# A list scheduler's prices: ScalarE, VectorE and GpSimd come free before an instruction's result, and exponentials are priced lower

## The chip, the cores and the metric

The kernel runs on one core of a Trainium2 chip. The metric is the device time of one execution in microseconds (us). TensorE (PE) multiplies matrices and loads its weights in a lane of its own (PEld); ScalarE (ACT), VectorE (DVE) and GpSimd (POOL) do elementwise work; SyncE (SP) only issues DMAs.

## What is computed

Local and global attention, then two MLP blocks, all in float32:

```python
scores = q @ k.T / sqrt(64) + bias               # 16 heads x 768 tokens, 8 global + 96 local keys
x = softmax(where(keep, scores, -1e9)) @ v
xk, xr = mu_k*x + (1-mu_k)*x_prev, mu_r*x + (1-mu_r)*x_prev
k = max(xk @ w_k, 0)                              # 512 -> 1024
x = sigmoid(xr @ w_r) * (k*k @ w_v)
xn = (x - mean) / sqrt(var + 1e-6) * g_ln
out = x + max(xn @ w_ch1, 0) @ w_ch2              # 512 -> 2048 -> 512
```

## The kernel before

The kernel has three stages. The **attention stage** (to about 148 us) goes through 12 blocks of 128 tokens, each in two halves of four heads. A half is: scores on PE (L484), four bias-and-minimum instructions on VectorE (L495, tile `t0l`), four exponentials on ScalarE (L501), transposes of the result on PE (L519), one copy `yy` on ScalarE (L337), and the product with the values on PE (L534), "values" below. Around each block PE also turns q and k (L438) and the reciprocal sums (L569); ScalarE copies the results (`b0h`, `xg`). In the same stage weights arrive by DMA and are converted and split into two float32r parts (L337, L341, L593 to L595, L601, L605), on ScalarE, VectorE and GpSimd. The first products of the first MLP, r (L720) and k of the first group (L756), can already run here, as fillers between the attention's PE work.

The **first MLP** (148 to about 282 us) is long runs of L756, L793 to L795 on PE. The **second MLP** (282 to 547 us) is 16 steps. A step has seven products P1 to P7 (L1047, six matmuls each, in the order P1 P6 P5 P7 P2 P4 P3) and three "down" groups of four operations (L1141 to L1143, three matmuls an operation). Between them, VectorE adds the products (L1055), ScalarE applies the ReLU and rounds the result to the high half of `h` (L1062, L337), and GpSimd makes the low half (L1066, four per step, called lows here; the fourth belongs to P3). A down group adds into banks 4 and 5 of PSUM, which VectorE's L1147 frees. In the even steps from 2 to 12 the weights of the next pair of steps are converted as well; on GpSimd that is a bundle of four small adds (L1000 to L1003) and two splits (L605) for each of two chunks.

The order of instructions on the four engines is not written by hand. `Plan.play` is a greedy list scheduler that runs when the program is built: it keeps a clock for each engine, and of all operations that can go it takes the one that can start first by these clocks; the due time only breaks ties. An operation names the engines that may do it with a price in ns on each; with two names, the engine that would finish first gets it, so prices also decide who does a conversion's copy (ScalarE 670 or GpSimd 850). A result may be used `LAG` = 70 ns after its end. Engines then run their instructions strictly in the order that came out. The lines that set a clock, and the price of an exponential:

```python
end = t + engines[e]
self.clock[e] = end
p.op({"ACT": 465 + 0.86 * w}, exp, ...)     # w = 128 or 232 columns
```

Of the kernel before, what the change touches and what calls it, by code (L numbers as in the profile page):

```python
# [51 lines left out]
def slope(h):  # L52
    return 2.0 ** (-8.0 * (h + 1) / H)
# [37 lines left out]
class Room:  # L91


    def __init__(self, tag, bufs, make, hold=False):
        self.tag, self.bufs, self.make, self.hold = tag, bufs, make, hold
        self.left, self.end, self.tile = 0, 0.0, None
# [13 lines left out]
class Plan:  # L110
# [4 lines left out]
    LAG = 70.0  # L115

    SWITCH = 95.0

    def __init__(self, clock):
        self.clock = {e: 1000.0 * t for e, t in clock.items()}  # L120
# [21 lines left out]
    def play(self):  # L142
        n = len(self.ops)
        wait = [len(x[2]) for x in self.ops]
        users = [[] for _ in self.ops]
        for i, x in enumerate(self.ops):
            for d in x[2]:
                users[d].append(i)
        ready = [0.0] * n
        by = {}  # L150
        free = {}
        live = {}
        open_ = [i for i in range(n) if not wait[i]]
        dma, mode = 0.0, ""
        trace = []
        while open_:
            best = None
            for i in open_:
                engines, _, _, rooms, due, _, _ = self.ops[i]
                at = ready[i]  # L160
                ok = True
                for x in rooms:
                    if x.tile is None:
                        if live.get(x.tag, 0) < x.bufs:
                            f = free.setdefault(x.tag, [0.0] * x.bufs)
                            at = max(at, f[0])
                        else:
                            ok = False
                if not ok:
                    continue  # L170
                for e, ns in engines.items():
                    t = max(at, self.clock[e])
                    if len(engines) > 1 and any(max(at, self.clock[g]) + m < t + ns for g, m in engines.items() if g != e):
                        continue
                    key = (t, due, i, e)
                    if best is None or key < best:
                        best = key
            if best is None:
                raise RuntimeError("no operation can go: " + str([(i, [x.tag for x in self.ops[i][3] if x.tile is None]) for i in open_][:20]))
            t, _, i, e = best  # L180
            engines, fn, _, rooms, _, size, way = self.ops[i]
            for x in rooms:
                if x.tile is None:
                    live[x.tag] = live.get(x.tag, 0) + 1
                    free[x.tag].pop(0)
                    x.tile = x.make()
            self.now = t
            fn(e)
            end = t + engines[e]
            if e == "PE" and way != mode:  # L190
                end += self.SWITCH
                mode = way
            self.clock[e] = end
            if size:
                dma = max(dma, end) + size / 190.0
                end = dma + 1900.0
            trace.append((t, end, e, i))
            for x in rooms:
                x.left -= 1
                x.end = max(x.end, end)  # L200
                if not x.left and not x.hold:
                    live[x.tag] -= 1
                    free[x.tag].append(x.end + self.LAG)
                    free[x.tag].sort()
            open_.remove(i)
            for u in users[i]:
                ready[u] = max(ready[u], end + self.LAG)
                wait[u] -= 1
                if not wait[u]:
                    open_.append(u)  # L210
        assert not any(wait), [i for i in range(n) if wait[i]][:20]
        return trace


class Fast:
# [247 lines left out]
    def plan_scores(self, i):  # L463


        nc, p = self.nc, self.plan
        n, hf = i // 2, i % 2
        c0, c1 = self.cols(n)
        w = c1 - c0
        banks = [Room(f"b{(2 * i + e) % 3}", 1, lambda e=e: self.bank((2 * i + e) % 3)) for e in range(2)]  # L470
        S = lambda k: banks[k % 2].tile[:, 0 : 2 * w].rearrange("p (j w) -> p j w", j=2)[:, k // 2, :]
        due = self.due(i)
        if hf == 0:
            self.sm[n] = self.room("sm", 3, [P, H])
        sm = self.sm[n]
        tp, mn = self.tp[i], _ = Part([self.TP, self.token(f"tp{i % 3}", 1)], lambda t, _: t[:, i % 3]), self.room("mn", 3, [P, 4])
        sides = [n % 2] if n % NB == 0 else [0, 1, 2]
        o = P + MAXG if n % 2 else 0
        s = hf if n == 0 else 0

        def scores(e):
            for k in range(4):
                r, c = slice((k % 2) * D, (k % 2 + 1) * D), 2 * hf + k // 2
                nc.tensor.matmul(S(k), self.qT(n)[r, c], self.kT()[r, c, c0:c1], start=True, stop=True)  # L484

        reads = self.sides(n, s, "qT", n % 2)
        for x in sides:
            reads += self.sides(n, s, "kT", x)
        p.op({"PE": 3.4 * w}, scores, reads, [("S", i)], banks + [self.Q, self.K], due, mode="rows")
        for x, k in enumerate((0, 2, 1, 3)):  # L490
            h = 4 * hf + k

            def least(e, k=k, h=h):
                bias = self.nb0 if n % NB == 0 else self.nb[:, o : o + WW]
                nc.vector.tensor_tensor_reduce(  # L495
                    tp.tile[:, k, 0:w], S(k), bias, slope(h), 3.0e38, ALU.add, ALU.min, mn.tile[:, k : k + 1]
                )

            def exp(e, k=k, h=h):
                t = tp.tile[:, k, 0:w]  # L500
                nc.scalar.activation(t, t, AF.Exp, bias=mn.tile[:, k : k + 1], scale=-1.0, accum_out=sm.tile[:, h : h + 1])  # L501

            p.op({"DVE": 165 + 1.31 * w}, least, [("S", i), ("nb", n % NB > 0)], [("tp", i, k)], [tp, mn, banks[k % 2], self.bias], due + 1 + x)
            p.op({"ACT": 465 + 0.86 * w}, exp, [], [("tp", i, k), ("sm", n, h)], [tp, mn, sm], due + 1.5 + x)

    def plan_weighted(self, i):

# [880 lines left out]
```

## Time and profile before

| | us |
|---|---|
| three timed runs | 554.62, 555.76, 554.92 (median 554.92) |
| the profiled execution | 556.07 |
| its span, first to last instruction | 554.2 |
| PE busy (3178 matmul records) | 528.0 (95%) |
| DVE, ACT, POOL busy | 403.8 (73%), 288.2 (52%), 278.6 (50%) |
| granted TensorE clock, mean | 0.989 |

The trace comes from the profiled execution, which took 1.15 us more than the median; 1.9 us of it lie outside the span. Times inside the trace count from the first instruction. A busy matmul is not a matmul at its peak, because matmuls overlap; so where PE's pace matters, the starts of two following instructions are compared, and not their durations.

### The profile page before, as it was taken

The page shows a single profiled execution, that of the slowest core. Times are in us where ns is not written, and L with a number is a line of the kernel's source. Part 1 is how long each engine was busy: PE and PEld are TensorE (multiplying, and loading weights), DVE is VectorE, ACT ScalarE, POOL GpSimd, SP SyncE. Part 2 cuts the span into 40 slices and gives each one's busy share as a digit, 9 for nine tenths or more (in the row PEclk, how much of TensorE's full clock was granted, in tenths as well). Part 3 has the DMA queues.
Part 4 walks back from the last instruction along what each step waited for, and adds up shares of the span by engine and source line. Part 5 has one row for each costly group of instructions (what it writes and reads, how often), then busy time and mean ns, then how long its engine had stood idle before and what let it go on. Part 6 is the DMA issues. An engine that isn't in the chain of part 4 may idle for free.

```text
span 554.2 us, 8779 instructions
## 1 busy us (share of the span) xinstructions
PE 528.0 (95%) x3178; PEld 454.2 (82%) x3178; DVE 403.8 (73%) x791; ACT 288.2 (52%) x641; POOL 278.6 (50%) x338
## 2 busy tenths in 40 slices
PE   5889999999999999999999999999999999999994
PEld 4667776887799898988888898788888889888983
DVE  4788799786597355828889987777676867867463
ACT  2687888777543313454446472473545526454320
POOL 3168575745545022151236592793855739585200
PEclk9699999999999999999999999999999999999999
DMA  8899667421310000020220123012130311311024
GB/s 168 205 229 192 150 157 176 146 69 53 101 38 2 1 2 0 1 72 5 77 69 8 52 63 95 20 64 90 45 109 0 115 39 43 110 38 39 0 77 157
DMA packets 59456, 42.64 MB, mean 77 GB/s; under 512 B 49036, under 2 KB 49292, under 8 KB 59404
## 3 DMA queue, kind: packets, MB, share of 16 engines
q1 hardware_dynamic: 58796, 41.33, 27.9%
q8 instruction: 27, 0.44, 0.3%
q10 hardware_dynamic: 576, 0.66, 0.3%
q14 instruction: 25, 0.20, 0.1%
q0 software_dynamic: 32, 0.00, 0.0%
HBM read 38.84 MB, written 3.15 MB: 76 GB/s over the span
## 4 chain that ended last, share of the span: by engine, by line


## 5 line engine op out<-in xcount | busy, mean ns | idle before, releaser
L1147 DVE TENSOR_TENSOR xg<-b,xg 128x1024 f32<-128x1024 f32 x44 | 53.6, 1219 | 39.5 <-PE b L1143 39.3
L595 DVE SCALAR_TENSOR_TENSOR cv<-cv,stage 128x512 int32<-128x512 int32 x50 | 43.9, 879 | 8.9 <-ACT cv L337 5.0
L594 DVE SCALAR_TENSOR_TENSOR stage<-stage 128x512 int32<-128x512 int32 x50 | 46.8, 938 | 0.6
L501 ACT ACTIVATE t0l<-t0l,mn 128x232 f32<-128x232 f32 (+1 forms) x96 | 44.5, 467 | 4.4 <-DVE mn L495 4.2
L1066 POOL TENSOR_TENSOR h<-rt,h 128x384 fp32r<-128x384 f32 x28 | 35.9, 1281 | 15.3 <-ACT h L337 15.3
L495 DVE CUSTOM_DVE_ANT_0 t0l<-b,ln 128x232 f32<-128x232 f32 (+1 forms) x96 | 32.0, 373 | 14.5 <-PE b L484 14.5
L664 POOL TENSOR_SCALAR rt<-xg,vec 128x256 f32<-128x256 f32 x48 | 29.9, 639 | 15.6 <-DVE m L771 4.3
L605 POOL TENSOR_TENSOR s<-cv,s 128x384 fp32r<-128x384 f32 (+1 forms) x22 | 26.8, 1217 | 19.0 <-ACT s L601 19.0
L1066 POOL TENSOR_TENSOR h<-e,h 128x384 fp32r<-128x384 f32 x14 | 15.9, 1134 | 38.2 <-ACT h L337 38.2
L831 POOL TENSOR_SCALAR st<-st 128x1 f32<-128x1 f32 x12 | 4.5, 375 | 60.2 <-DVE st L828 60.0
L756 PE MATMUL b<-b0l,t1l 128*128 128x256 f32 x144 | 32.6, 284 | 0.5 <-DVE rt L766 0.5
L593 DVE TENSOR_SCALAR stage<-stage 128x512 int32<-128x512 int32 x50 | 30.9, 620 | 2.8 <-DMA stage<-in_moe_w_v_dram 1.6
L519 PE MATMUL b<-ident,t0l 128*116 128x128 f32 (+1 forms) x176 | 30.1, 287 | 1.5 <-ACT t0l L501 1.5
L669 DVE SCALAR_TENSOR_TENSOR rt<-xg,vec,rt 128x256 f32<-128x256 f32 x48 | 29.1, 654 | 1.4 <-POOL rt L664 1.4
L1062 ACT ACTIVATE e<-e 128x384 f32<-128x384 f32 x16 | 8.3, 522 | 41.5 <-DVE e L1055 41.5
L534 PE MATMUL b<-yy,h 116*64 116x128 f32 (+1 forms) x352 | 25.0, 283 | 4.8 <-ACT yy L337 4.8
L1047 PE MATMUL b<-t1h,s 128*128 128x384 f32 x128 | 27.8, 339 | 0.6 <-DVE e L1055 0.6
L1062 ACT ACTIVATE rt<-rt 128x384 f32<-128x384 f32 x32 | 16.6, 520 | 22.6 <-DVE rt L1055 22.6
L534 PEld LDWEIGHTS b<-yy,h 116*64 116x64 f32 (+1 forms) x352 | 19.0, 138 | 11.2 <-ACT yy L337 8.6
L337 ACT ACTIVATE yy<-b 116x1024 f32<-116x1024 f32 (+1 forms) x24 | 22.8, 949 | 10.0 <-PE b L519 9.9
L1047 PE MATMUL b<-t0h,s 128*128 128x384 f32 x128 | 27.9, 339 | 0.0
L519 PEld LDWEIGHTS b<-ident,t0l 128*116 128x116 f32 (+1 forms) x176 | 20.1, 139 | 8.5 <-issue 3.8
(307 smaller groups left out, 1673.4 us busy)
## 6 DMA issues: line engine op xcount, KB each, us to landing
stage<-in_moe_w_ch_dram SPq DMA_DIRECT2D x32, 512.0 KB
stage<-in_moe_w_k_dram SPq DMA_DIRECT2D x8, 512.0 KB
stage<-in_moe_w_v_dram SPq DMA_DIRECT2D x8, 512.0 KB
h<-in_v_dram SPq DMA_DIRECT2D x10, 192.0 KB
b0l<-in_q_dram SPq DMA_DIRECT2D x7, 256.0 KB
out_dram<-xg SPq DMA_DIRECT2D x3, 512.0 KB
stage<-in_moe_w_r_dram SPq DMA_DIRECT2D x2, 512.0 KB
b0h<-in_q_dram SPq DMA_DIRECT2D x4, 256.0 KB
```

The costliest lines, as they stand in the source:

```text
L495: nc.vector.tensor_tensor_reduce(tp.tile[:, k, 0:w], S(k), bias, slope(h), 3.0e38, ALU.add, ALU.min, mn.tile[:, k : k + 1])
L501: nc.scalar.activation(t, t, AF.Exp, bias=mn.tile[:, k : k + 1], scale=-1.0, accum_out=sm.tile[:, h : h + 1])
L519: nc.tensor.transpose(b.tile[0:w, c, k * P : (k + 1) * P], tp.tile[:, k, c * w : (c + 1) * w], self.ident)
L534: nc.tensor.matmul(o, self.V[n].tile[0:w, c, h, :], y.tile[0:w, c, k * P : (k + 1) * P], start=c == 0, stop=c == m - 1)
L593: p.op({"DVE": 500}, lambda e: nc.vector.tensor_scalar(low(), low(), 29, None, ALU.logical_shift_right), [R], [(R, 1)], [raw], due - 2, be ...
L594: p.op({"DVE": 760}, lambda e: nc.vector.scalar_tensor_tensor(low(), high(), -(1 << 31), low(), ALU.bitwise_and, ALU.bitwise_or), [R, (R, ...
L595: p.op({"DVE": 760}, lambda e: nc.vector.scalar_tensor_tensor(y(), y(), 3, low(), ALU.logical_shift_left, ALU.bitwise_or), [(R, 2)], [C], ...
L664: nc.gpsimd.tensor_scalar(y.tile[:, u], z, v, 0.0, ALU.mult, ALU.add)
L756: nc.tensor.matmul(o, l, r, start=s == 0, stop=s == 11)
L1047: nc.tensor.matmul(acc(x), lhs(i, c, n), rhs(r, j, c), start=y == 0, stop=y == 5)
L1066: lambda e: (nc.vector if e == "DVE" else nc.gpsimd).tensor_tensor(o(1), V(y), o(0).bitcast(F32), ALU.subtract),
L1147: p.op({"DVE": 1250}, lambda e, x=x, z=rooms[0]: nc.vector.tensor_tensor(x(), z.tile.rearrange("p a n -> p (a n)"), x(), ALU.add), cells, ...
```

## The change

Two prices change and nothing else. After an operation, the clock of ScalarE, VectorE or GpSimd is set back by 105, 85 or 120 ns from the operation's end; the result still counts as ready at the end. And an exponential is priced 80 ns lower.

```diff
     SWITCH = 95.0
+    OVERLAP = {"ACT": 105.0, "DVE": 85.0, "POOL": 120.0}
...
-            self.clock[e] = end
+            self.clock[e] = end - self.OVERLAP.get(e, 0.0)
...
-            p.op({"ACT": 465 + 0.86 * w}, exp, [], [("tp", i, k), ("sm", n, h)], [tp, mn, sm], due + 1.5 + x)
+            p.op({"ACT": 385 + 0.86 * w}, exp, [], [("tp", i, k), ("sm", n, h)], [tp, mn, sm], due + 1.5 + x)
```

The same operations are built, 2142 in number; what moves is their order, on every engine, and for 22 operations the engine: 18 of them are copies of a weight conversion, ten from ScalarE to GpSimd and eight the other way. PE's 654 operations keep 89 changes between its kinds of work. Three places follow. In the changed kernel every line after 117 has a number one higher.

**Place 1: PE in the attention stage, around block 6's first scores.** Before, transposes of half 10 (L519), the turn of k for block 6 (L438), its scores (L484), another turn, then the values of half 10 (L534):

```order
L438 MATMUL b3_126_840<-ident_60,u_12_128 128x128 x4
L519 MATMUL b45_125_829<-ident_60,t0l_24_190 116x128 x2
L484 MATMUL b0_129_857<-b0h_15_139,b0l_11_126 128x128
L484 MATMUL b1_130_858<-b0h_15_139,b0l_11_126 128x128
...
L438 MATMUL b3_131_863<-ident_60,b0l_11_126 128x128 x4
L534 MATMUL b6_134_881<-yy_34_228,h1_13_135 64x128 x8
```

The same place of the changed kernel:

```order
L520 MATMUL b45_125_836<-ident_60,t0l_24_190 116x128 x6
L721 MATMUL b7_126_845<-s0_33_231,h0_70_463 128x512 x6
L439 MATMUL b3_130_863<-ident_60,u_12_128 128x128 x4
...
L520 MATMUL b45_125_836<-ident_60,t0l_24_190 116x128 x2
L485 MATMUL b0_131_888<-b0h_15_139,b0l_11_126 128x128
L485 MATMUL b1_132_889<-b0h_15_139,b0l_11_126 128x128
...
L721 MATMUL b7_134_899<-s0_33_231,h0_70_463 128x512 x6
L535 MATMUL b6_137_915<-yy_35_242,h1_13_135 64x128 x8
```

The r products of group 1 (L721), which stood some forty operations later before, now lie between these transposes, scores and values. All r and first k products are used up earlier: the last of them stands 27 places of PE's 654 earlier, and the last five halves of the attention have none between their operations.

**Place 2: PE in the second MLP, between the last down group of step 2 and the first of step 3.** Before, from the last matmul of step 2 (tile `h1_463`): P2 and P4 of step 4 (L1047), then step 3's first down operation (tile `h1_491`):

```order
L1143 MATMUL b45_489_3704<-b0r_325_2450,h1_463_3514 128x512
L1047 MATMUL b2_490_3719<-b0h_352_2685,s0_349_2668 128x384 x4
L1047 MATMUL b2_490_3719<-b0l_383_2975,s0_349_2668 128x384 x2
L1047 MATMUL b3_492_3732<-t0h_327_2468,s0_349_2668 128x384 x4
L1047 MATMUL b3_492_3732<-t0l_330_2481,s0_349_2668 128x384 x2
L1141 MATMUL b45_494_3747<-b1h_390_3041,h1_491_3726 128x512
L1142 MATMUL b45_494_3747<-yy_409_3171,h1_491_3726 128x512
L1143 MATMUL b45_494_3747<-b1h_390_3041,h1_491_3726 128x512
```

The same place of the changed kernel:

```order
L1144 MATMUL b45_484_3670<-b0r_325_2450,h1_461_3488 128x512
L1048 MATMUL b6_486_3690<-b0h_352_2678,s0_349_2665 128x384 x4
L1048 MATMUL b6_486_3690<-b0l_383_2976,s0_349_2665 128x384 x2
L1048 MATMUL b7_488_3703<-t0h_327_2468,s0_349_2665 128x384 x4
L1048 MATMUL b7_488_3703<-t0l_330_2478,s0_349_2665 128x384 x2
L1048 MATMUL b0_489_3713<-t0h_327_2468,s0_349_2665 128x384 x4
L1048 MATMUL b0_489_3713<-t0l_330_2478,s0_349_2665 128x384 x2
L1048 MATMUL b1_490_3721<-t0h_327_2468,s0_349_2665 128x384 x4
L1048 MATMUL b1_490_3721<-t0l_330_2478,s0_349_2665 128x384 x2
L1142 MATMUL b45_493_3733<-b1h_390_3043,h1_487_3697 128x512
L1143 MATMUL b45_493_3733<-yy_412_3181,h1_487_3697 128x512
L1144 MATMUL b45_493_3733<-b1h_390_3043,h1_487_3697 128x512
```

Four products (P1, P6, P5, P7 of step 4) instead of two now stand between the end of step 2 and step 3's first down operation. Step 2's last group itself stands four products earlier than before, and in later steps too the down groups follow their step's products more closely: in steps 8 and 12 the third down operation, which needs the low of P3, comes after P1, a down operation, P6, a down operation, P5 and P7.

**Place 3: GpSimd in step 8, ahead of the low of P3.** Before, the bundle of the first chunk and then the low (L1066):

```order
L1003 TENSOR_TENSOR stage_557_4216<-cv_574_4333,stage_557_4216 128x128
L605 TENSOR_TENSOR s1_395_3074<-cv_574_4333,s1_395_3074 128x384
L605 TENSOR_TENSOR s1_395_3074<-stage_557_4216,s1_395_3074 128x512
L1066 TENSOR_TENSOR h0_572_4319<-rt_569_4303,h0_572_4319 128x384
L1000 TENSOR_TENSOR stage_561_4253<-cv_581_4408 128x128
```

The same place of the changed kernel:

```order
L1004 TENSOR_TENSOR stage_557_4221<-cv_575_4347,stage_557_4221 128x128
L606 TENSOR_TENSOR s1_395_3081<-cv_575_4347,s1_395_3081 128x384
L342 TENSOR_SCALAR cv_583_4422<-stage_562_4267 128x512
L606 TENSOR_TENSOR s1_395_3081<-stage_557_4221,s1_395_3081 128x512
L1067 TENSOR_TENSOR h0_573_4333<-rt_570_4317,h0_573_4333 128x384
L1001 TENSOR_TENSOR stage_562_4267<-cv_583_4422 128x128
```

The copy of the next chunk (L342, by ScalarE before) now stands on GpSimd ahead of the low of P3. The same is so in steps 6, 10 and 12.

## Rows read from the trace of the kernel before

**Rows 1.** Busy time by stretch: us, five engines (x instructions), PE clock, DMA share, GB/s.
```profile
20.00:40.00 20.00, 16.18 (x142) 11.62 (x140) 16.21 (x50) 15.85 (x45) 8.18 (x11) 0.93 1.01 209
40.00:150.00 110.00, 104.84 (x877) 83.37 (x874) 85.99 (x242) 84.74 (x228) 70.46 (x81) 1.00 0.52 132
150.00:300.00 150.00, 149.54 (x910) 133.43 (x910) 108.71 (x196) 65.07 (x120) 49.60 (x73) 1.00 0.09 27
300.00:360.00 60.00, 57.50 (x290) 50.91 (x289) 49.07 (x69) 29.05 (x57) 37.38 (x40) 1.00 0.18 53
360.00:545.00 185.00, 184.10 (x904) 163.58 (x903) 130.84 (x178) 85.96 (x170) 107.62 (x111) 1.00 0.20 64
```

**Rows 2.** PE's waits: waiting line <- releaser: us in total, times, longest us.
```profile
PE b L534 <- ACT yy L337: 4.8, 8, 0.9
PE b L1047 <- DVE e L1055: 1.5, 2, 0.9
```

**Rows 3.** Timeline, attention stage, three engines: start us, us, engine, line, tiles, shapes, [idle before].
```profile
114.35 1.02 ACT L337 ACTIVATE yy<-b 116x1024 f32<-116x1024 f32 x1
115.26 0.49 ACT L501 ACTIVATE t0l<-t0l,mn 128x232 f32<-128x232 f32 x1
...
115.73 0.49 ACT L501 ACTIVATE t0l<-t0l,mn 128x232 f32<-128x232 f32 x1
...
64.06 0.40 DVE L495 CUSTOM_DVE_ANT_0 t0l<-b,ln 128x232 f32<-128x232 f32 x1
64.38 0.08 DVE L495 DVE_READ_ACCUMULATOR2_ANT mn<- 128x1 f32 x1
...
40.69 0.69 POOL L341 TENSOR_SCALAR cv<-stage 128x512 f32<-128x512 f32 x1
41.33 0.60 POOL L562 COPY xg<-sm 128x512 f32<-128x512 f32 x1
```

**Rows 4.** Timeline of PE, attention stage.
```profile
68.99 0.72 PE L484 MATMUL b<-b0h,b0l 64*128 64x128 f32 x8 [0.45 <-ACT b0h L337]
...
71.19 1.09 PE L534 MATMUL b<-yy,h 116*64 116x128 f32 x16 [0.90 <-ACT yy L337]
...
83.99 0.66 PE L534 MATMUL b<-yy,h 128*64 128x128 f32 x8 [0.69 <-ACT yy L337]
...
87.33 1.05 PE L484 MATMUL b<-b0h,b0l 64*128 64x232 f32 x8 [0.45 <-ACT b0h L337]
...
147.30 1.09 PE L534 MATMUL b<-yy,h 116*64 116x128 f32 x16 [0.85 <-ACT yy L337]
```

**Rows 5.** Timeline of PE, and one row of ACT, start of the second MLP.
```profile
315.04 0.93 PE L1047 MATMUL b<-t1h,s 128*128 128x384 f32 x4 [0.65 <-DVE e L1055]
...
337.87 0.50 PE L1141 MATMUL b<-b0h,h 128*128 128x512 f32 x1 [0.58 <-DVE xg L1147]
...
353.58 0.49 PE L1143 MATMUL b<-b1h,h 128*128 128x512 f32 x1 [0.37 <-POOL h L1066]
...
356.30 0.98 PE L1047 MATMUL b<-b1h,s 128*128 128x384 f32 x4 [0.87 <-DVE e L1055]
...
349.30 0.63 ACT L601 ACTIVATE b0h<-cv 128x512 fp32r<-128x512 f32 x1 [8.70 <-PE b L1143]
```

**Rows 6.** Timeline of POOL, step 8 of the second MLP.
```profile
423.76 1.02 POOL L1066 TENSOR_TENSOR h<-g,h 128x384 fp32r<-128x384 f32 x1
...
426.73 1.47 POOL L605 TENSOR_TENSOR s<-cv,s 128x384 fp32r<-128x384 f32 x1
...
429.41 1.47 POOL L1066 TENSOR_TENSOR h<-rt,h 128x384 fp32r<-128x384 f32 x1
```

**Rows 7.** Timeline of PE, from step 9's P1 over one down group.
```profile
424.97 0.85 PE L1047 MATMUL b<-b1h,s 128*128 128x384 f32 x4
...
426.02 0.39 PE L1141 MATMUL b<-b1h,h 128*128 128x512 f32 x1
...
428.79 0.87 PE L1047 MATMUL b<-t1h,s 128*128 128x384 f32 x4
```

## The prediction

> **What bounds the kernel now.** I read the busy time by stretch first. PE is busy for 104.84 of the 110 us from 40 to 150, 149.54 of the next 150, 57.50 of the 60 from 300 to 360 and 184.10 of the 185 up to 545 [rows 1]. So PE sets the time nearly everywhere, and an order of instructions can give back only PE's waits: 3.8 us in the 20 us from 20 to 40 (where the granted clock is still 0.93 and DMAs take all of their share, 1.01), 5.2 us in the rest of the attention stage, 2.5 us at the start of the second MLP, and 0.5 and 0.9 us in the two long stretches [rows 1]. PE's work itself is unchanged, down to the number of changes of kind.
>
> Second come the waits by releaser: eight waits of the values product for ScalarE's yy copy make 4.8 us, two waits of an up product for VectorE's adds 1.5 us [rows 2]. These two are the kinds to follow through the new order. VectorE is the next engine: 85.99 of 110 us in the attention stage and 49.07 of 60 from 300 to 360 [rows 1]. Where it is that full, a PE wait that goes may come back a little later as a wait for VectorE.
>
> **Do the new prices fit?** An instruction's start and end, and the next one's start, show the overlap that the change speaks of. On ScalarE the yy copy runs from 114.35 to 115.37 and the next instruction starts at 115.26: 0.11 us. Two exponentials start 0.47 us apart (115.26 and 115.73) [rows 3]. The old price of one was 465 + 0.86 x 232 = 665 ns of the engine's time; the new one, 585 - 105 = 480 ns, is right to 0.01 us. On VectorE 64.06 + 0.40 against 64.38 is 0.08 us of overlap, as the change has it, and the minimum takes 0.32 us of the engine against 469 ns in the old plan and 384 in the new [rows 3]. On GpSimd 40.69 + 0.69 against 41.33 is 0.05 us [rows 3], not 0.12. So two of three engines become truer, and GpSimd is now believed to be free about 0.07 us too early after each instruction. The new plan thinks ScalarE and VectorE faster than the old one did, and so puts PE's work earlier behind them.
>
> **The change part by part.** *20 to 40 us.* PE's waits here change places (the values of half 2 follow the transposes with one turn between, where scores stood before; scores that waited now come after values). No wait can be said to go without another coming; I take 0, with 0.8 us (two waits of about 0.4) either way.
>
> *40 to 148 us, waits that go.* At 68.99 and 71.19 PE waits 0.45 us for the scores' input and 0.90 us for yy [rows 4]. In the new order r products stand in both gaps (place 1). An r half takes 1.6 us or so of PE, more than either wait. At 83.99 (0.69 us) scores and a turn now both stand ahead of the values, and at 87.33 (0.45 us) r products and values stand ahead of the scores [rows 4]. These four make 2.5 us. The price of filling early is that the last five halves have no filler.
>
> *Waits that come.* Values now follow their transposes with only a turn between in half 5, and with nothing between in half 22, where something longer stood before. The nearest rows are the values that had just four transposes ahead: 0.85 us at 147.30 and 0.90 us at 71.19 [rows 4]. The yy copy alone is 1.02 us [rows 3], so 0.9 us is a fair price and 1.2 us the upper bound; two of them make 1.8 us. Net for the stage: -0.7 us. Bounds: -3.3 us (all four go, none comes, and 20 to 40 gives its 0.8) and +2.6 us (none of the four is a net gain, and 1.8 + 0.8 come).
>
> *148 to 300 us.* The order differs in two short pieces, among products that are all ready; PE is busy for 149.54 of 150 us [rows 1]: 0.
>
> *300 to 360 us, waits that go.* Four waits make 0.65 + 0.58 + 0.37 + 0.87 = 2.47 us [rows 5]. The first and the last are up products that wait for VectorE to empty a bank; the second is a down group that waits for L1147. In the new order VectorE does the last norm of the second half of the tokens some ten instructions earlier, L1147 stands ahead of the next weight conversion and not behind two thirds of it, and adds stand between the parts of a conversion. The third (place 2) is a low that GpSimd delivers late: ScalarE's split at 349.30 had stood 8.70 us waiting for PE to finish with the old weights, and the rounding of h is queued behind it; the low comes 353.58 - 349.30 = 4.3 us after that split starts [rows 5]. The split starts about 1.2 us before step 2's last group ends. Now four products of 1.05 us [rows 7] follow that group, not two, so PE has 1.2 + 4.2 = 5.4 us of work until the low is needed: enough. VectorE stays 49.07 of 60 us busy, and not every wait behind it will vanish; I take -2.0 us, between -2.5 and 0.
>
> *360 to 545 us, waits that come.* In step 8 the low of P3 ends at 429.41 + 1.47 = 430.88, which is 5.9 us after the next step's P1 starts (424.97) [rows 6, 7]. The new order needs it after four products of 1.05 us and two down operations of 2.77 / 4 = 0.69 us [rows 7], that is 5.6 us after P1 starts, and puts a copy of 0.64 us of GpSimd's time [rows 3] ahead of it (place 3). So PE waits 5.9 + 0.64 - 5.6 = 0.95 us there. Step 12 has the same order, another 0.95. In steps 6 and 10 a whole down group stands ahead, 6.6 us after P1: 0.1 us together. That is +2.0 us; the 0.9 us that PE waits in this stretch now [rows 1] belong to an order that is gone, so +1.1 us net, bounds -0.9 and +5.
>
> Here a rule of the Trainium skill speaks against the change. The rows: the same low, 128x384, takes 1.02 us at 423.76 and 1.47 us at 429.41 [rows 6], so a flat price less 120 ns is 0.06 us short of the quick one and 0.5 us short of the slow one. The page "SBUF — State Buffer" (Who interferes with whom) says that VectorE and GpSimd share a port pair that is held for a whole instruction, so that the other "fully blocks"; VectorE's two-input instructions collide with GpSimd's reads. By it each collision costs GpSimd some half a microsecond that no plan of this kind knows; the second rival is what follows if it strikes in more steps.
>
> **Sum.** 0 - 0.7 + 0 - 2.0 + 1.1 = -1.6 us. The profiled execution's 556.07 would become 554.5; the profile sits 1.15 us above the median of the runs, so against that median, 554.92, it is **553.3 us**.
>
> **The rivals.** *The plan is simply truer* and nearly all waits that it can reach go: 0.8 + 2.5 + 2.5 us, with no new ones behind yy or GpSimd; 554.9 - 5.8 = 549.1. For it: ScalarE and VectorE's prices match to 0.01 to 0.06 us. Against it: the two thin places behind yy are in the order, whatever the price.
>
> *GpSimd too late* (the slower side): the bundle ahead of a low of P3 runs from 424.74, the end of the low before less the overlap, to 430.88, 6.1 us [rows 6]; the new prices give it 1680 + 960 + 1320 + 960 = 4.9 us. From the point where the low comes later than 5.6 us after P1, each of the six even steps from 2 to 12 loses what is missing, up to 1.2 us, and not only steps 8 and 12. Six waits of 1.0 us instead of my 2.0 us add 4.0: 553.3 + 4.0 = 557.3.
>
> *Fillers eaten too early* (no change): the last five halves of the attention have only their own PE work. ScalarE has four exponentials of 0.47, a yy copy of 0.9 and a share of other copies per half, nearly as much as PE. If PE waits 0.3 us more in each of these, the stage's gain is gone and 0.8 us more with it: 553.3 + 1.5 = 554.8.
>
> *The change does not do what it says*: the orders differ, but waits only change places everywhere, as they do from 20 to 40 us: 554.9.
>
> **How the numbers follow.** Chances: my forecast 0.38, the truer plan 0.12, fillers too early 0.16, only changed places 0.10, GpSimd too late 0.24. A measurement of this kernel can tell about 0.2%, or 1.1 us, from no change, so faster means below 553.8. Three quarters of the forecast's chance and all of the truer plan's lie there, and a quarter of the two that lead to no change: 0.29 + 0.12 + 0.06 = 0.47. Slower (above 556.0) is the GpSimd rival and a little of fillers too early: 0.28. The rest, 0.25, is no change. The range reaches from the truer plan, 549.1, to the GpSimd rival, 557.3. Alone, the forecast's own case spans 551 to 555.
>
> **What the profile of the changed kernel would show.** Right: the waits of 0.90 and 0.69 us for yy gone between 66 and 88 us, r products standing there; waits of 0.8 us or more for yy at halves 5 and 22; PE busy for about 59.5 of the 60 us from 300 to 360; waits of PE for L1067 of about 1 us in steps 8 and 12. Wrong: PE waits for L1067 in every even step (the GpSimd rival); PE's busy share falling well below nine tenths from 125 to 148 us (fillers); or, from 300 to 360, the same 2.5 us with other names.

## The result, and the profile after

The changed kernel is slower: 561.75 us median (561.51 to 561.85, 4 runs) against 555.33 us for the kernel before (554.62 to 555.76, 4 runs). The ratio is 1.0113, 95% interval 1.0098 to 1.0128. The prediction was 553.3 us, with a range from 549.1 to 557.3; both the sign and the size are wrong, and the time lies outside the range.

Busy time by stretch of the kernel after (us; five engines with their instructions; granted TensorE clock; DMA share; GB/s), to be held against [rows 1]:

```profile
20.00:40.00 20.00, 18.20 (x149) 13.55 (x148) 17.29 (x51) 16.44 (x50) 10.86 (x15) 0.88 1.01 203
40.00:150.00 110.00, 100.63 (x822) 80.13 (x818) 90.86 (x245) 85.85 (x225) 70.79 (x76) 0.98 0.58 140
150.00:300.00 150.00, 148.00 (x925) 132.06 (x926) 100.69 (x184) 62.37 (x114) 44.34 (x72) 1.00 0.07 22
300.00:360.00 60.00, 58.28 (x298) 52.61 (x297) 46.49 (x72) 31.24 (x62) 34.64 (x38) 1.00 0.17 53
360.00:545.00 185.00, 182.31 (x901) 163.08 (x900) 132.15 (x178) 86.06 (x170) 110.76 (x119) 1.00 0.18 58
```

In the second row PE is idle for 9.4 us of 110, where it had been idle for 5.2. VectorE is busier than before there, 90.86 against 85.99 us. Mapped to the operations, the attention stage's last values end at 154.7 us instead of 148.4, and the second MLP then takes 264.1 us from its first up product to its last down group, where it took 264.5. So the whole loss is made in the attention stage. These two windows hold the same PE work, of before and of after, up to the end of those last values:

```profile
0.00:148.40 148.40, 133.33 (x1067) 103.71 (x1067) 112.06 (x346) 107.31 (x295) 82.44 (x114) 0.97 0.64 149
```

```profile
0.00:154.70 154.70, 134.15 (x1067) 105.13 (x1067) 121.33 (x355) 112.59 (x303) 88.87 (x120) 0.96 0.67 151
```

PE's idle time grows from 15.1 to 20.6 us, and its busy time by 0.8 us at a slightly lower mean clock (0.96 in place of 0.97): 5.5 + 0.8 = 6.3 us. Where in the stage? I added PE's gaps of over 0.2 us, half by half (the halves are numbered from 0 to 23). Halves 0 to 13 have 8.5 us before and 8.3 after. Halves 14 to 23 have 1.6 us before and 7.9 after. Up to half 13 the change is even a little ahead, with ten filler operations done where the kernel before had done six. PE's timeline after, the waits of the attention stage from 42 us on that matter (start, duration, ..., [idle before <- releaser]):

```profile
42.25 1.09 PE L535 MATMUL b<-yy,h 116*64 116x128 f32 x16 [0.74 <-ACT yy L338]
57.44 1.09 PE L535 MATMUL b<-yy,h 116*64 116x128 f32 x16 [0.96 <-ACT yy L338]
89.79 0.43 PE L520 MATMUL b<-ident,t0l 128*116 128x128 f32 x2 [0.92 <-ACT t0l L502]
91.54 0.63 PE L570 MATMUL b<-ident,xg 128*128 128x128 f32 x4 [1.32 <-DVE b0l L446]
92.86 1.07 PE L439 MATMUL b<-ident,b0h 128*128 128x128 f32 x4 [0.47 <-ACT xg L338]
124.13 1.09 PE L535 MATMUL b<-yy,h 116*64 116x128 f32 x16 [1.63 <-ACT yy L338]
150.01 1.09 PE L535 MATMUL b<-yy,h 116*64 116x128 f32 x16 [1.17 <-ACT yy L338]
```

The four waits of [rows 4] between 66 and 88 us are gone, as forecast. The waits at 42.25 and 150.01 are the two that the prediction named. The rest was not in it: a jam of 2.7 us at 90 us, 1.63 us at 124 us, and smaller ones.

What happened at 90 us is on VectorE and GpSimd. VectorE's and GpSimd's timeline there, then two conversion steps of VectorE a little later, while GpSimd stood idle:

```profile
84.52 2.03 DVE L670 SCALAR_TENSOR_TENSOR rt<-xg,vec,rt 128x256 f32<-128x256 f32 x2
...
84.83 1.43 POOL L606 TENSOR_TENSOR t1l<-cv,t1l 128x512 fp32r<-128x512 f32 x1
...
86.99 2.94 POOL L677 TENSOR_TENSOR h<-rt,h 128x512 fp32r<-128x512 f32 x2
...
87.11 1.69 DVE L595 SCALAR_TENSOR_TENSOR stage<-stage 128x512 int32<-128x512 int32 x1
...
88.72 0.39 DVE L496 CUSTOM_DVE_ANT_0 t0l<-b,ln 128x232 f32<-128x232 f32 x1
...
89.04 1.43 DVE L596 SCALAR_TENSOR_TENSOR cv<-cv,stage 128x512 int32<-128x512 int32 x1
...
90.40 0.39 DVE L496 CUSTOM_DVE_ANT_0 t0l<-b,ln 128x232 f32<-128x232 f32 x1
...
94.20 0.68 DVE L595 SCALAR_TENSOR_TENSOR stage<-stage 128x512 int32<-128x512 int32 x1
...
94.99 0.69 DVE L596 SCALAR_TENSOR_TENSOR cv<-cv,stage 128x512 int32<-128x512 int32 x1
```

The same two steps, L595 and L596, take 1.69 and 1.43 us while GpSimd works and 0.68 and 0.69 us while it does not. Two of the four minimums of a half (L496) stand behind them in VectorE's row, their exponentials behind the minimums, and PE's transposes behind the exponentials. At 124 us it is the same kind of chain, one link longer, and it starts at an instruction that is not a conversion step:

```profile
117.28 2.85 DVE L670 SCALAR_TENSOR_TENSOR rt<-xg,vec,rt 128x256 f32<-128x256 f32 x2
...
120.71 0.47 ACT L502 ACTIVATE t0l<-t0l,mn 128x232 f32<-128x232 f32 x1
...
123.07 1.00 ACT L338 ACTIVATE yy<-b 116x1024 f32<-116x1024 f32 x1
```

L670 takes 2.85 us for two beside GpSimd's L606 and L772 (1.21 us for two at 83.05); the next half's minimums come late, so its exponentials start at 120.71. The copy yy of the half before, whose input was ready at about 121.1, is queued on ScalarE behind all four of them and starts only at 123.07.

### The profile page after: what moved, and what is told of

Same layout as the page of the kernel before. It is cut to its first block, busy times and chain, and to the rows that moved or that the text cites. A ratio compares the mean times of both kernels' runs of the same rounds, so it can differ in the third digit from the quotient of the medians.

```text
span 559.9 us, 8813 instructions
## 1 busy us (share of the span) xinstructions
PE 527.2 (94%) x3178; PEld 456.5 (82%) x3178; DVE 404.5 (72%) x791; ACT 288.8 (52%) x639; POOL 275.7 (49%) x340
## 4 chain that ended last, share of the span: by engine, by line
## 5 line engine op out<-in xcount | busy, mean ns | idle before, releaser
L1148 DVE TENSOR_TENSOR xg<-b,xg 128x1024 f32<-128x1024 f32 x44 | 53.7, 1220 | 36.8 <-PE b L1144 36.4
L596 DVE SCALAR_TENSOR_TENSOR cv<-cv,stage 128x512 int32<-128x512 int32 x50 | 45.1, 902 | 9.1 <-POOL cv L342 4.6
L595 DVE SCALAR_TENSOR_TENSOR stage<-stage 128x512 int32<-128x512 int32 x50 | 44.6, 891 | 0.6
L1067 POOL TENSOR_TENSOR h<-rt,h 128x384 fp32r<-128x384 f32 x28 | 34.0, 1216 | 18.8 <-ACT h L338 18.8
L496 DVE CUSTOM_DVE_ANT_0 t0l<-b,ln 128x232 f32<-128x232 f32 (+1 forms) x96 | 31.7, 372 | 11.0 <-PE b L485 10.9
L606 POOL TENSOR_TENSOR s<-cv,s 128x384 fp32r<-128x384 f32 (+1 forms) x22 | 24.9, 1130 | 19.7 <-ACT s L602 19.6
L520 PE MATMUL b<-ident,t0l 128*116 128x128 f32 (+1 forms) x176 | 28.8, 285 | 3.8 <-ACT t0l L502 3.8
L594 DVE TENSOR_SCALAR stage<-stage 128x512 int32<-128x512 int32 x50 | 31.4, 627 | 1.0 <-DMA stage<-in_moe_w_ch_dram 1.0
L670 DVE SCALAR_TENSOR_TENSOR rt<-xg,vec,rt 128x256 f32<-128x256 f32 x48 | 29.9, 670 | 1.1 <-POOL rt L665 1.1
L721 PE MATMUL b<-s,h 128*128 128x512 f32 x96 | 27.6, 425 | 0.6 <-ACT g L726 0.6
```

Source lines behind the costliest of these rows:

```text
L496: nc.vector.tensor_tensor_reduce(tp.tile[:, k, 0:w], S(k), bias, slope(h), 3.0e38, ALU.add, ALU.min, mn.tile[:, k : k + 1])
L520: nc.tensor.transpose(b.tile[0:w, c, k * P : (k + 1) * P], tp.tile[:, k, c * w : (c + 1) * w], self.ident)
L594: p.op({"DVE": 500}, lambda e: nc.vector.tensor_scalar(low(), low(), 29, None, ALU.logical_shift_right), [R], [(R, 1)], [raw], due - 2, be ...
L595: p.op({"DVE": 760}, lambda e: nc.vector.scalar_tensor_tensor(low(), high(), -(1 << 31), low(), ALU.bitwise_and, ALU.bitwise_or), [R, (R, ...
L596: p.op({"DVE": 760}, lambda e: nc.vector.scalar_tensor_tensor(y(), y(), 3, low(), ALU.logical_shift_left, ALU.bitwise_or), [(R, 2)], [C], ...
L670: nc.vector.scalar_tensor_tensor(y.tile[:, u], z, v, y.tile[:, u], ALU.mult, ALU.add)
```

## The experiments

Three theories. **Short prices**: the new prices leave out the time that GpSimd costs VectorE, so the plan runs ahead of the chip and puts operations in orders that the chip can't follow. **Fillers**: the r and k products are used up too early. **Scatter**: any other order than that of before is slower by chance. Ratios are to the kernel before, with 95% intervals.

### The stage: two halves of the change

The new prices apply only before (`e_att`), or only after (`e_rest`), the last values of the attention stage are placed (`on` starts as true in the one and as false in the other; operation 525 is those values):

```diff
-            end = t + engines[e]
+            end = t + engines[e] - (80 if on and way == "exp" else 0)
...
-            self.clock[e] = end - self.OVERLAP.get(e, 0.0)
+            self.clock[e] = end - (self.OVERLAP.get(e, 0.0) if on else 0.0)
+            if i == 525:
+                on = not on
```

> New prices and the new order up to the last values of the attention stage, old prices from there on. The two traces put the attention's end 6.3 us later (148.4 against 154.7 us) and the kernel's end 6.3 us later too, so all theories of the attention stage (short prices, fillers spent early, one jam) expect the whole loss here: 561 to 562 us. If the later stages took part, it would be 558 or less.

> Old prices and the old order up to the last values of the attention stage, new prices from there on. By the theories of the attention stage the time is the old one, 555, give or take 1 us: the trace after has 264.1 us from the second MLP's start to its last down group, before 264.5. My prediction gave this part -0.9 us (waits of 2.0 us gone up to 360 us, 1.1 us new behind it), so 554.4; the rival that GpSimd comes too late gave +2 or more, 557.

Measured: `e_att` 563.15 us, 1.0143 (1.0110 to 1.0177); `e_rest` 555.28 us, 1.0014 (0.9997 to 1.0031). The loss of the change is in the attention stage, and the gain of 0.9 us that I forecast for the second MLP is not to be seen.

### One price at a time

`e_exp` has only the exponential's price, `e_act` that and ScalarE's overlap, `e_dve` only VectorE's overlap, `e_pool` only GpSimd's:

```diff
-    OVERLAP = {"ACT": 105.0, "DVE": 85.0, "POOL": 120.0}
+    OVERLAP = {"DVE": 85.0}
```

> Only the exponential's price, 80 ns lower; no overlap. ScalarE's old sum for the attention stage, 122.7 us, is 23 us above the chip's 99.6; this takes 7 us of it away and leaves VectorE's and GpSimd's prices, whose sums fit (110.2 against 101.1, 80.3 against 77.2). Short prices: no loss, 554 to 556 us. Fillers spent early: this order has none in the last four halves either, as after, so 560 to 562.

> ScalarE's overlap of 105 ns and the exponential's price; VectorE and GpSimd as of old. ScalarE's sum is then 96.5 against the chip's 99.6 us. Short prices: the engine whose new sum fits does no harm, 554 to 556 us. Fillers spent early: none in the last three halves, so a loss of some 4 us, 559.

> Only VectorE's overlap of 85 ns. VectorE's sum falls from 110.2 to 94.0 us where the chip took 101.1. Short prices: this is the part that does most of the harm, 558 to 562 us. Fillers spent early: none in the last two halves only, a small loss, 556 to 557.

> Only GpSimd's overlap of 120 ns. GpSimd's sum falls from 80.3 to 71.0 us where the chip took 77.2; but GpSimd is busy for 85 of 110 us and seldom the last. Short prices: a small loss, 555.5 to 557 us. Fillers spent early: none in the last four halves, 560 to 562. My prediction's rival (GpSimd believed free too early) would give the loss of the change, above 560, here alone.

| | us | ratio | interval |
|---|---|---|---|
| `e_exp` | 564.63 | 1.0171 | 1.0135 to 1.0207 |
| `e_act` | 559.14 | 1.0070 | 1.0034 to 1.0106 |
| `e_dve` | 564.96 | 1.0178 | 1.0146 to 1.0210 |
| `e_pool` | 563.51 | 1.0154 | 1.0113 to 1.0194 |

Each part alone loses, three of them more than all together. Short prices in the form that I had written it (the sum of an engine's prices) is wrong for `e_exp`, `e_act` and `e_pool`, which leave VectorE's sum as it was, and `e_dve` lies above its range too. Fillers is right for `e_act` alone and far off for `e_dve`. (GpSimd, in the expectation of `e_pool`, is busy for 70.46 of the 110 us [rows 1], and not for 85.) A new theory was needed that explains why even a price that becomes truer does harm; or it was scatter.

The jam is not the same in each. In `e_exp` the worst wait is 4.09 us of PE, behind a VectorE that stands still for a weight load; SyncE's, VectorE's and PE's timelines there:

```profile
104.27 3.13 SPq L418 DMA_DIRECT2D h<-in_v_dram  x2
...
107.50 0.35 SPq L590 DMA_DIRECT2D stage<-in_moe_w_v_dram  x1
...
111.87 0.43 DVE L593 TENSOR_SCALAR stage<-stage 128x512 int32<-128x512 int32 x1 [2.94 <-DMA stage<-in_moe_w_v_dram]
...
117.54 0.50 PE L756 MATMUL b<-s,t1l 128*128 128x256 f32 x2 [4.09 <-DVE rt L766]
```

The load was issued at 107.50, behind two loads of another tile in SyncE's row, and VectorE's in-order row waits for it with everything that stands behind.

Nor is it always in the attention stage. `e_pool` ends that stage at 149.2 us, 0.8 us later than before, and loses in the second MLP, which takes 271.3 us in place of 264.5. Its down groups wait there for VectorE's L1148 five times, 6.0 us in all, and for GpSimd's lows, which my rival asked for, only 0.7 us. At the longest of these waits L1148 stands behind a whole conversion that runs beside GpSimd; VectorE's and PE's timelines:

```profile
369.58 1.17 DVE L594 TENSOR_SCALAR stage<-stage 128x512 int32<-128x512 int32 x1
...
370.78 1.67 DVE L595 SCALAR_TENSOR_TENSOR stage<-stage 128x512 int32<-128x512 int32 x1
...
372.56 1.30 DVE L596 SCALAR_TENSOR_TENSOR cv<-cv,stage 128x512 int32<-128x512 int32 x1
...
373.77 1.21 DVE L1148 TENSOR_TENSOR xg<-b,xg 128x1024 f32<-128x1024 f32 x1
...
375.04 0.50 PE L1142 MATMUL b<-b0h,h 128*128 128x512 f32 x1 [2.62 <-DVE xg L1148]
```

From 369.58 to 373.77 the conversion holds VectorE for 4.19 us, where its three prices are 2.02 us. `e_act` and `e_dve` lose a part in the second MLP as well, which takes 267.2 and 268.0 us there.

### Fillers held back

New prices, but a filler may go only when as many halves are done as before it in the old order:

```diff
             for i in open_:
+                if halves < self.HOLD.get(i, 0):
+                    continue
```

> New prices, but no filler (r or k product) may go before as many halves of the attention are done as it had before it in the old order. Fillers spent early: the loss of halves 14 to 22 goes, 555 to 557 us. Short prices: the plan still believes VectorE 7 us and GpSimd 6 us quicker than they are, and the waits of PE stay, with fewer fillers to cover the first halves: 561 or more.

Measured: 559.58 us, 1.0084 (1.0058 to 1.0109), between the two expectations. The median lies 2.2 us below that of the change, but by the ratios only a quarter of the loss goes, and the intervals overlap: that the fillers have a part is possible and not shown. The runs below settle the rest: an order that uses its fillers as early as the change does need not lose.

### Measured prices

`e_fit` keeps the new overlap and sets 27 lines of prices so that price less overlap is what the chip took in the trace of before. What an operation took of its engine is counted from its start to the next one's start, or to its end where the engine then waits. In the attention stage, from 20 us on, in ns (the prices themselves go by the mean over the whole program, 625 + 920 + 870 for a conversion):

| VectorE, ScalarE | chip | old price | new price less overlap |
|---|---|---|---|
| conversion, three steps (18 times) | 625 + 944 + 739 | 500 + 760 + 760 | 415 + 675 + 675 |
| minimum (88) | 315 | 457 | 372 |
| exponential (88) | 493 | 656 | 471 |

```diff
-        p.op({"DVE": 500}, lambda e: nc.vector.tensor_scalar(low(), ...
-        p.op({"DVE": 760}, lambda e: nc.vector.scalar_tensor_tensor(low(), ...
-        p.op({"DVE": 760}, lambda e: nc.vector.scalar_tensor_tensor(y(), ...
+        p.op({"DVE": 710}, lambda e: nc.vector.tensor_scalar(low(), ...
+        p.op({"DVE": 1005}, lambda e: nc.vector.scalar_tensor_tensor(low(), ...
+        p.op({"DVE": 955}, lambda e: nc.vector.scalar_tensor_tensor(y(), ...
...
-            p.op({"DVE": 165 + 1.31 * w}, least, ...
+            p.op({"DVE": 108 + 1.31 * w}, least, ...
...
-                {"DVE": 570} if k in (0, 2 * PAIRS - 1) else {"POOL": 1080},
+                {"DVE": 570} if k in (0, 2 * PAIRS - 1) else {"POOL": 1330},
```

> The new overlap stays, but 20 prices are set so that price less overlap is the mean time that the operation held its engine in the trace of before (VectorE's conversion 710, 1005, 955 instead of 500, 760, 760 ns; the minimum 108 instead of 165 + 1.31 w; GpSimd's lows 1330 instead of 1080). Short prices: the harm of the change is that its VectorE sums to 94.0 us where the chip took 101.1 and its GpSimd to 71.0 where the chip took 77.2; with both right the loss goes, 555 us or less, and the plan's own time of the attention's end differs from the chip's by under 4 us, against 14.2 after. Fillers spent early: this order has none in the last three halves and 10 in halves 15 to 18, so it loses about half, 558. One jam: any other order gets rid of it, 555 to 556.

Measured: 549.76 us, 0.9893 (0.9852 to 0.9935), faster than both kernels. The plan still ran ahead of the chip, by 7.1 us at the last values, more than the 4 I expected; the size of the plan's error is not what decides.

### Controls: the same prices, another order

Each price of VectorE, ScalarE and GpSimd off by up to 2% by the operation's number, in two patterns (389, and 617 in its place):

```diff
         i = len(self.ops)
+        near = 1 + 0.02 * (2 * (i * 389 % 1009) / 1008 - 1)
+        engines = {e: ns * (near if e in ("ACT", "DVE", "POOL") else 1) for e, ns in engines.items()}
```

> A control: the prices of before, each operation of ScalarE, VectorE and GpSimd off by up to 2% either way by its number, so that every sum stays and only ties and near ties fall otherwise. Short prices alone: nothing true is lost, so 554 to 556 us. Lucky order (the order of before is one in many of its kind, and any other of the same prices is slower, which would explain why each part alone lost 5 to 10 us): 558 to 565.

> The same control with another pattern of up to 2%. Short prices alone: 554 to 556 us. Lucky order: 558 to 565, and not the same as the first pattern.

> The measured prices (overlap kept, 20 prices raised to the chip's means) off by up to 2% either way. Short prices: the gain comes from prices that are right, so it stays, 548 to 552 us. Lucky order: the 549.8 of the measured prices was one draw, and this one lies with the others, 556 to 565.

> The measured prices with the other pattern of up to 2%. Short prices: 548 to 552 us. Lucky order: 556 to 565.

| | us | ratio | interval |
|---|---|---|---|
| `j_before1` | 558.47 | 1.0060 | 1.0037 to 1.0084 |
| `j_before2` | 555.08 | 1.0001 | 0.9979 to 1.0023 |
| `j_fit1` | 550.46 | 0.9917 | 0.9893 to 0.9941 |
| `j_fit2` | 555.46 | 1.0023 | 0.9990 to 1.0055 |

Neither theory gets all four. Scatter is real: a change of prices that means nothing moves the time by 0.6% (`j_before1`) or takes the gain of the measured prices away (`j_fit2`). From `e_fit` to `j_fit2` it is 1.3%, as much as the loss of the change, so no single order proves anything here; only a set of them does. None of these four reaches the least of the single parts, 1.0070, but the intervals of that one (`e_act`) and of `j_before1` overlap.

### Only the conversion's three prices

`e_conv` is the change with 710, 1005 and 955 for the three steps of a conversion and nothing else corrected; `j_conv2` the same with the second pattern; `j_after2` the change with the second pattern; `e_expconv` is `e_exp` with 625, 920 and 870.

> The change as it is, and in addition the three VectorE prices of a conversion at the chip's means plus the overlap: 710, 1005, 955 instead of 500, 760, 760 ns. Nothing else is corrected. Short prices of the conversion: most of the loss goes, 552 to 556 us. Scatter: anything from 553 to 565. A loss through GpSimd's or ScalarE's prices: 560 to 562, as the change.

> The same with each price off by up to 2% by the second pattern. Short prices of the conversion: 552 to 557 us again. Scatter: not the same as the unjittered one, by several us.

> The change with each price off by up to 2% by the second pattern. Short prices: the loss stays, 559 to 564 us. Scatter: the 561.7 was one bad draw, and this lies at 553 to 558.

> No overlap; the exponential's new price, and the three VectorE prices of a conversion at the chip's means, 625, 920, 870 instead of 500, 760, 760 ns. Short prices of the conversion: the exponential's price alone cost 9 us because the old one, 160 ns too high, had covered for them; with them right the time is 553 to 557. Rival (the exponential's price by itself spoils the order, whatever VectorE is believed to take): 561 or more.

| | us | ratio | interval |
|---|---|---|---|
| `e_conv` | 555.31 | 1.0019 | 1.0001 to 1.0036 |
| `j_conv2` | 552.83 | 0.9964 | 0.9948 to 0.9979 |
| `j_after2` | 560.41 | 1.0105 | 1.0081 to 1.0128 |
| `e_expconv` | 554.58 | 1.0017 | 0.9989 to 1.0044 |

Three prices take the loss away, twice in the change and once beside the exponential's price, and the change's loss stays in size under a new pattern. It does not stay in place: `j_after2` ends the attention stage at 150.1 us, only 1.7 us later than before, and its second MLP takes 267.3 us. Four waits of 0.98 or 0.99 us stand there behind L1148 (L1150 in that kernel), and each time two conversion steps of some 1.25 and 1.77 us stand just ahead of it. In `e_conv` no filler is left for the last four halves either, as in the change, and yet it loses next to nothing: early fillers are not the cause by themselves. The window from 40 to 150 us of `e_conv`:

```profile
40.00:150.00 110.00, 104.66 (x873) 83.18 (x872) 87.42 (x248) 92.85 (x240) 64.17 (x72) 1.00 0.58 141
```

PE is busy for 104.66 us, as before (104.84), and not 100.63. At 86 us VectorE now does the four minimums of a half in one go, with the conversion behind them and not between them. (The next half's are still parted, one at 89.19 and three from 92.19 on, but by L670, L446 and L576 and not by conversion steps.)

```profile
86.13 0.40 DVE L496 CUSTOM_DVE_ANT_0 t0l<-b,ln 128x232 f32<-128x232 f32 x1 [0.62 <-PE b L485]
...
86.45 0.39 DVE L496 CUSTOM_DVE_ANT_0 t0l<-b,ln 128x232 f32<-128x232 f32 x1
...
86.77 0.40 DVE L496 CUSTOM_DVE_ANT_0 t0l<-b,ln 128x232 f32<-128x232 f32 x1
...
87.09 0.40 DVE L496 CUSTOM_DVE_ANT_0 t0l<-b,ln 128x232 f32<-128x232 f32 x1
...
87.41 0.43 DVE L594 TENSOR_SCALAR stage<-stage 128x512 int32<-128x512 int32 x1
```

### GpSimd's overlap

`e_poolconv` is `e_pool` with the conversion's prices at 625, 920 and 870; `e_conv_nopool` is `e_conv` without GpSimd's 120 ns.

> GpSimd's overlap of 120 ns alone, with the conversion's three VectorE prices at the chip's means (625, 920, 870). Short prices of the conversion: the 8.5 us that the overlap alone cost go, 553 to 557 us. GpSimd believed free too early (my prediction's rival): they stay, 560 or more, as a wait of the down groups in the second MLP.

> The change with the conversion's three prices corrected, as the run that gave 555.3 us, and no overlap on GpSimd, where the trace shows only 0.04 us of it. GpSimd believed free too early: 2 us or more below the 555.3. Short prices of the conversion alone: 553 to 557.

Measured: `e_poolconv` 557.62 us, 1.0043 (1.0014 to 1.0073), just above the range of its expectation; `e_conv_nopool` 554.75 us, 0.9994 (0.9977 to 1.0010). With the conversion priced right, some seven tenths of what GpSimd's overlap cost alone goes, and its second MLP takes 265.1 us in place of 271.3; the rest lies within the scatter of the controls. Taking the overlap out of the corrected change moves the median by 0.6 us and the ratio by 0.25%, some 1.4 us, and not by 2 or more: GpSimd believed free too early is at most a small part of the cause.

## Why the prediction was wrong, point by point

**What it takes together.** In eight orders prices are lowered and the conversion's stay at 500, 760 and 760 (the change, `j_after2`, `e_att`, `e_hold` and the four single parts); they are 0.7 to 1.8% slower than before, 1.3% on average. In eight others the conversion's are set to what the chip takes (`e_fit`, `j_fit1`, `j_fit2`, `e_conv`, `j_conv2`, `e_expconv`, `e_poolconv`, `e_conv_nopool`); they lie between 1.1% faster and 0.4% slower, 0.2% faster on average. The ratios of the two sets do not overlap, though their members are relatives and not independent draws, and the intervals at the border do (`e_act`, `e_poolconv`). What the losing orders share is the price and not the place: where the long waits were followed back, here at 90 us, in `e_pool` and in `j_after2`, something that PE needs stood in VectorE's row behind conversion steps that took 1.2 to 1.8 us each. The old prices were short for the conversion too (2020 ns against 2308), but 142 ns too high for each minimum and 163 for each exponential, four of each in a half. In the attention stage from 20 us on, VectorE's old prices sum to 110.2 us and the chip took 101.1; the new ones less overlap sum to 94.0. I read this as errors of opposite sign that covered for each other; no run lowers the minimum alone. The plan's own times fit it but do not prove it. Before, it put the last values at 145.7 us and the chip began them at 147.3; after, it put them at 139.4 and the chip began them at 153.6; yet the plan of `e_fit`, off by 7.1 us, gains.

**The step that failed** is "Do the new prices fit?". It compared the new prices with the chip for a copy, the exponential and the minimum, and concluded that "two of three engines become truer". It never did so for the conversion, VectorE's largest piece of work in the stage. So the term for 40 to 148 us came out at -0.7 us with an upper bound of +2.6, where the stage lost 6.3. The page of the profile before had the means, 620, 938 and 879 ns for L593, L594 and L595, against prices of 500, 760 and 760 that the change lowers by 85 more. The durations of the three on the kernel before (min/median/max ns) show why a mean of the quick ones misleads:

```profile
L593 DVE TENSOR_SCALAR stage<-stage x50: 389/454/1447, 13.1 to 504.2; 128x512 int32<-128x512 int32 x50
L594 DVE SCALAR_TENSOR_TENSOR stage<-stage x50: 642/692/1686, 16.5 to 505.5; 128x512 int32<-128x512 int32 x50
L595 DVE SCALAR_TENSOR_TENSOR cv<-cv,stage x50: 634/692/1596, 17.3 to 506.2; 128x512 int32<-128x512 int32 x50
```

The new prices less overlap, 415, 675 and 675, are the time of a conversion beside an idle GpSimd to within 20 ns (411 to 431, 674 to 695 and 673 to 694 ns in that trace). They are right for an engine that works alone.

**The rule that the prediction weighed, and used on the wrong engine.** It took half a microsecond of collision for GpSimd's lows. The rows above show the other side, VectorE's conversion steps at 1.69 and 1.43 us. The Trainium skill, "SBUF — State Buffer" (Who interferes with whom), says that a VectorE instruction with two SBUF inputs contends with a GpSimd instruction that reads SBUF, and that whoever comes second waits; the trace agrees for the two steps with two inputs in SBUF, and so it does for an instruction that the page leaves alone: L1148, which reads PSUM, takes 1.21 to 1.23 us whether GpSimd works or not. The first step has one input, so the rule on two inputs does not reach it, and it too goes from 0.39 to 1.45 us in the row of L593 above.

**The terms.** *20 to 40 us*, 0: the values of half 4 end at 38.6 us in place of 39.3, so it held within its 0.8 us. *40 to 148 us*, -0.7: the four waits went (2.5 us) and the two came (0.74 and 1.17 us, forecast 0.9 each), but the stage lost 6.3 us, by waits that do not follow from PE's order, because what PE waits for is late on VectorE. The upper bound of +2.6 had no term for it. *300 to 360 us*, -2.0: PE is busy for 58.28 us, not 59.5, so -0.8. *360 to 545 us*, +1.1: PE's idle time rises by 1.8 us. Steps 8 and 12 do wait for the low of P3, as forecast, but 0.44 and 0.45 us and not 0.95 each; two waits for VectorE's L1148, 0.9 us each, were not forecast. From its first up product to its last down group the second MLP gains 0.4 us, where the two terms together had 0.9. Its waits after, from 300 to 545 us (in total, times, longest):

```profile
PE b L1142 <- DVE xg L1148: 3.5, 4, 1.1
PE b L1144 <- POOL h L1067: 0.9, 2, 0.4
```

**The rivals.** *The plan is simply truer*: false for the change, since it was truer only for engines that work alone; with prices that hold what the engines cost each other its time is nearly reached (`e_fit`, 549.8, against 549.1 for the rival), but only in two of three draws. *GpSimd too late* gave the nearest time of all, 557.3, with the wrong mechanism: lows were late for 0.9 us in all. *Fillers eaten too early* may be a part, at most a third of the loss by `e_hold` (2.2 us, priced at 1.5), but in another place: of the 6.3 us of idle time that came after half 13, halves 14 to 18 have 4.8 and the last four, which have no filler left (four, and not the five that I counted), 1.4. *Only changed places*: false, since 6.3 us of PE's time were lost.

**What stays open.** A single order's time has scatter that no theory here predicts, from 0.1% to 1.3% between draws of the same prices, so what each of the other 24 lines of `e_fit` is worth can't be told. One rival is untested: that any VectorE price raised by as much, and not the conversion's, would have taken the loss away. The wait at 124 us starts at L670 and not at a conversion step; that `e_conv` does not have it may be another draw. Why `e_exp` and `e_dve` lose more than the whole change is not settled beyond the waits seen in them; the late load in `e_exp` is not a conversion's price, and that `e_expconv` does not have it may be another draw too.

## What to carry to other kernels

Prices in a planner are a set: before one is made truer, compare all that share an engine with the mean that the chip took, contention included, because a price that is too high may cover for one that is too low. An instruction's time alone is not its price where two engines slow each other; take the mean over the real program, and look at the min, median and max of each group. And run a few meaningless perturbations of the prices before believing a gain or loss of about a per cent from a new order.

## What was not expected of the hardware

TensorE's granted clock in the first 40 us differs between executions of the same order, and moves the whole time. The kernel before and `e_rest` have the same order up to the last values of the attention stage; their windows from 0 to 40 us:

```profile
0.00:40.00 40.00, 30.08 (x200) 21.68 (x202) 27.14 (x107) 23.34 (x69) 13.58 (x36) 0.87 0.98 201
```

```profile
0.00:40.00 40.00, 28.70 (x229) 21.12 (x231) 29.94 (x116) 26.02 (x75) 15.95 (x40) 1.00 0.95 193
```

At a granted clock of 1.00 (the upper level, 2.4 GHz) in place of 0.87 (in part at the lower, 1.2 GHz), 229 matmuls are done in place of 200, and the last values of the attention stage end at 145.3 us in place of 148.4. And a jam costs more than its wait: behind the idle time at 90 us the granted clock of the changed kernel fell below 1.00, where it had been 1.00 in both of these stretches of the kernel before:

```profile
90.00:95.00 5.00, 3.21 (x15) 2.49 (x14) 4.89 (x17) 4.11 (x11) 2.08 (x2) 0.80 0.83 171
95.00:100.00 5.00, 5.00 (x36) 3.52 (x34) 0.89 (x2) 2.61 (x8) 3.95 (x5) 0.86 0.96 243
```
